# Batch 0's values: stationary columns read in steps of 64 elements in place of a sorted copy, with another order of work around it

## The chip, the cores and the metric

One core of a Trainium2 chip runs the whole kernel. The metric is device time in microseconds of one execution. A core has a matrix engine (TensorE, "PE" in the profile, with its weight loads on a row of their own, "PEld"), VectorE ("DVE"), ScalarE ("ACT"), GpSimd ("POOL", which here also issues the loads from DRAM) and SyncE ("SP"). Each engine runs its own instructions in the order written; semaphores make it wait for the others. Products of TensorE land in PSUM banks of 2 KB a partition, from which ScalarE or VectorE copies them out.

## What is computed

Two parts in a row: an attention whose key and value blocks are mixed by a doubly normalised 8x8 matrix, and a token and channel mixing network on its output.

```python
batch, n_heads, seq, head_dim = (4, 8, 768, 64)          # 8 blocks of 96
P = sort_net                                             # (4, 8, 8, 8)
for _ in range(5):
    P = np.exp(P - np.max(P, axis=-1, keepdims=True))
    P = P / (np.sum(P, axis=-1, keepdims=True) + 1e-09)
    P = P / (np.sum(P, axis=-2, keepdims=True) + 1e-09)
k_sorted = np.einsum('bhij,bhjcd->bhicd', P, k_b)
v_sorted = np.einsum('bhij,bhjcd->bhicd', P, v_b)
scores = scale * np.matmul(q_b, k_sb.transpose(0, 1, 2, 4, 3))   # within a block
attn = softmax(scores);  x = attn @ v_sb                 # back to (4, 768, 512)

a1 = alpha1 * x + beta1
tok = np.einsum('ts,bsd->btd', w_tok, a1)                # w_tok 768x768
u = x + lam * tok
a2 = alpha2 * u + beta2
ch = np.maximum(a2 @ w_ch1, 0.0) @ w_ch2                 # 512x2048, 2048x512
out = u + lam * ch
```

## The kernel before

The kernel works on one batch after another. From batch 1 on, a batch's attention is woven into the channel products of the batch before it. Batch 0 has nothing to hide behind: its attention is written out by hand, instruction by instruction, and this is where the change lies. A wrapper around each engine keeps the program's order on that engine, so the text of the first order (lines 893 to 957) is the order in which each engine meets the work. All instructions are recorded under the wrapper's line 65 in the profile, so tiles, not lines, tell what an instruction is.

Up to the first product of the channel network (tile `h_ps`) batch 0 goes as follows.

- **Loads.** GpSimd issues q, k, v, `w_tok`, then `alphaB`, `betaB`, `lamB`, four parts of `W1p`, four of `W2p`, and later (`load_kv(1)`, line 959, `load_q(1)`) the raw v and k of batch 1 and its six parts of q (`qn`). k and v take the two buffers of tag "raw"; `KT0` (turned keys) and `VD` (sorted values) take those of tag "tw".
- **The mixing matrix.** Five rounds of normalisation on VectorE and ScalarE. Beside them TensorE turns q (`q_ps`) and runs fillers: `warm(n)` (line 229) issues n products of zeros, whose result nobody reads. `mask(n)` (line 211) makes small constant masks on VectorE, in rounds 0 to 2.
- **Keys.** `mix_keys` (line 327) spreads the matrix over partitions (`repk_ps`) and makes `bigK` in two halves on VectorE. `k_turn` (line 392) multiplies it into the keys, one pair of heads at a time, and `k_copy` (line 395) brings the result into `KT0`.
- **Values.** `v8` holds, on each partition, 48 tokens of 64 elements. `v_sort` (line 167) copies it into `VD`, 64 elements of 64 tokens each (48 and zeros): elements 16 to 32 and 48 to 64 on GpSimd, 0 to 16 on ScalarE, 32 to 48 on VectorE. `v_mix` (line 403) makes eight elements at a time: 16 products, each with one element's 64 token columns of `VD` as the stationary operand and `bigV` as the moving one. A filler into the same bank stands before each even one. The result goes to `Vs`.
- **Attention.** `score` (line 419) makes the products of half a pair of heads into two PSUM banks and one exp of 128x768 into `et`. `pv_first` (line 453) multiplies with `Vs` (`x_ps`, 24 products), and VectorE takes the reciprocal (`rc`) and scales into `x`.
- **Token weights.** `permute` (line 594) reorders half of `w_tok` (`wt`) into `wp` with two copies (1,728 and 576 elements a partition; in before the first half is split in two). `wtok` turns it on TensorE (`wtok_ps`) and copies it into `w_tokT`.
- **First half of the tokens.** `row_sum(m)` adds up rows of `w_tok` on ScalarE into `rcol`; `row_sums` (line 613) copies `rcol` to `rc`, turns it on TensorE (`rr_ps`), and ScalarE copies the result into the row `rrow`. `first_mm(g)` (line 665) is the token product of column group g (`tok_ps`, 6 products) and ScalarE's copy `tok`. `first_turn(g)` (line 677) turns x (three products), adds the outer product of `rrow` and `brow` as a fourth (`turn_ps`); ScalarE then makes `z`, and VectorE, in `first_finish` (line 654), makes `a2T` from `tok_ps` and `z`. The `h_ps` products need the four `a2T`.

PSUM is given out by two helpers: `psa` (two buffers of two banks) and `psb` (four buffers of one bank).

Of the kernel before, what the change touches and what calls it, by code (L numbers as in the profile page):

```python
# [7 lines left out]
FT = mybir.dt.float32  # L8
F16 = mybir.dt.float16
# [7 lines left out]
def kernel(  # L17
# [75 lines left out]
    def const(shape, dtype, name):  # L93
        return wts.tile(shape, dtype, name=name, tag=name)
# [13 lines left out]
    nc.sync.dma_start(bet1[:], moe_beta1.rearrange("(o c) -> o c", o=1))  # L108

    KT0 = att.tile([128, H4, NB, 128], F16, name="kT0", tag="tw", bufs=2)  # L110
    VD = att.tile([128, D, 64], F16, name="vd", tag="tw", bufs=2)
    Vs = const([128, H * NB, GRP], F16, "Vs")
    q8 = moep.tile([128, H4, 12 * D], F16, name="q8", tag="u16", bufs=1)
    k8 = att.tile([128, H4, 12 * D], F16, name="k8", tag="raw", bufs=2)
    v8 = att.tile([128, HB, D], F16, name="v8", tag="raw", bufs=2)

    def load_slabs(dst, src):
        flat = src[0].rearrange("h s d -> (h s d)").rearrange("(g p f) -> p g f", p=128, f=12 * D)
        for g in range(0, H4, 2):
            pool.dma_start(dst[:, g:g + 2, :], flat[:, g:g + 2, :])  # L120

    def load_halves(dst, src):
        for th in range(2):
            pool.dma_start(
                dst[th * 64:(th + 1) * 64, :, :],
                src.rearrange("h (j th t) d -> th (h j) t d", j=NB, th=2)[th],
            )
# [10 lines left out]
    brow = att.tile([128, C], F16, name="brow", tag="uT", bufs=2)  # L138
    rrow = att.tile([128, 384], F16, name="rrow", tag="uT", bufs=2)
    load_slabs(q8, q)  # L140
    ident16 = const([128, 128], F16, "ident16")
    pool.memset(ident16[:], 0.0)
    pool.affine_select(
# [3 lines left out]
    dve.memset(brow[:].bitcast(FT), 0.0)  # L147
    dve.memset(rrow[:].bitcast(FT), 0.0)
    load_slabs(k8, k)
    load_halves(v8, v[0])  # L150
    heads()
    wt16 = []
    for half in range(2):
        t_ = att.tile([128, 3, S], F16, name="wt16", tag=("sums", "qn")[half], bufs=(2, 1)[half])
        for lo, n in ((0, 96), (TAIL, 32)):
            pool.dma_start(
                t_[lo // 6:lo // 6 + n],
                moe_w_tok[lo + 3 * half * n:lo + 3 * (half + 1) * n, :].rearrange("(tt p) s -> p tt s", p=n),
            )
        wt16.append(t_)  # L160
        if half == 0:
            pool.memset(VD[:, :, HB:64], 0.0)
            pool.memset(
                KT0[:].rearrange("p g i (th t) -> p (g i th) t", th=2)[:, :, HB:64].bitcast(FT), 0.0
            )

    def v_sort(lo, hi, eng):
        eng(VD[:, lo:hi, 0:HB], v8[:, :, lo:hi].rearrange("p t d -> p d t"))

    W1p = const([128, CT, HID], BF, "W1p")  # L170
    W2p = const([128, HT, C], F16, "W2p")
# [2 lines left out]
    alphaB = const([128, C], F16, "alphaB")  # L174
    betaB = const([128, C], F16, "betaB")
    lamB = att.tile([128, C], FT, name="lamB", tag="kT", bufs=1)
    pool.dma_start(alphaB[:], moe_alpha1.partition_broadcast(128))
    pool.dma_start(betaB[:], moe_beta1.partition_broadcast(128))
    pool.dma_start(lamB[:], moe_lam.partition_broadcast(128))
    v_sort(16, 32, pool.tensor_copy)  # L180
    for g in range(4):
        if g == 1:
            v_sort(48, 64, pool.tensor_copy)
        pool.dma_start(W1p[:, :, g * 512:(g + 1) * 512], w1v[:, :, g * 512:(g + 1) * 512])
    pool.tensor_tensor(brow[0:1, :], bet1[:], lam1[:], ALU.mult)

    vscr = dram.tile([B, H * NB, BLK, D], F16, name="vscr", tag="vscr")
    raw_of = {}
    qn_of = {}
# [21 lines left out]
    def mask(n):  # L211
        if n == 0:
            dve.tensor_copy(ident16f[:], ident16[0:4 * CT, 0:4 * CT])
            dve.tensor_reduce(mlo[:], ident16[:].rearrange("p (b j) -> p j b", j=NB), AXX, ALU.add)
        elif n == 1:
            dve.tensor_reduce(msk[:], ident16[:].rearrange("p (b j) -> p b j", j=NB), AXX, ALU.add)
            dve.tensor_tensor(mhi[:], msk[:, 0:8], msk[:, 8:16], ALU.add)
            dve.tensor_reduce(mth[:], ident16[:].rearrange("p (th c) -> p th c", th=2), AXX, ALU.add)
        elif n == 2:
            dve.tensor_reduce(  # L220
                mgap[:], ident16[:].rearrange("p (th t) -> p th t", th=2)[:, :, 0:HB],
                mybir.AxisListType.XY, ALU.add,
            )
# [5 lines left out]
    def warm(n, ps=psa):  # L229
        fill(ps([128, 512], FT, "warm_ps")[:], n)  # L230
# [71 lines left out]
    for it in range(5):  # L302
        act.activation(P32[:], P32[:], AF.Exp)
        dve.tensor_reduce(rsum[:], P32[:], AXX, ALU.add)
        dve.reciprocal(rsum[:], rsum[:])
        dve.tensor_tensor(
            P32[:], P32[:], rsum[:].unsqueeze(2).to_broadcast([BH, NB, NB]), ALU.mult
        )
        dve.tensor_reduce(csum[:], P32[:].rearrange("p i j -> p j i"), AXX, ALU.add)
        dve.reciprocal(csum[:], csum[:])  # L310
        dve.tensor_tensor(
            (P16 if it == 4 else P32)[:], P32[:],
            csum[:].unsqueeze(1).to_broadcast([BH, NB, NB]), ALU.mult,
        )
        if it < 3:
            with nc.allow_low_precision(reason="sums of zeros and a one"):
                mask(it)
        for f in beside[it]:
            f()

    for g in range(4):
        pool.dma_start(W2p[:, g * 4:(g + 1) * 4, :], w2v[:, g * 4:(g + 1) * 4, :])

    bigK = {}
    bigV = {}
# [66 lines left out]
    def k_turn(b, g, ps):  # L392
        return turn_slab(k8, lambda r, g: bigK[b][r, g, :], g, "k_ps", ps)
# [9 lines left out]
    def v_mix(b, n, ps, eng):  # L403
        ps = ps([128, 8, 64], FT, "v_ps")
        fill(ps[:].rearrange("p d x -> p (d x)"), 1 - n % 2)
        for s in range(8):
            for th in range(2):
                d = (s + 4 * th) % 8
                r = slice(th * 64, th * 64 + 64)
                pe.matmul(  # L410
                    ps[r, d, :], VD[r, n * 8 + d, :],
                    bigV[b][r, :, :].rearrange("p h i -> p (h i)"), start=True, stop=True,
                )
        eng(Vs[:, :, n * 8:(n + 1) * 8], ps[:].rearrange("p d x -> p x d"))
# [2 lines left out]
    kT_of = {0: KT0}  # L417

    def score(b, g, hf, ps):
        ps = ps([128, 2, 512], FT, "sc_ps")  # L420
        n = 128 if b == 0 else BLK
        keys = kT_of[b][:].rearrange("p g i t -> p (g i t)")
        for ii in range(4):
            i = 4 * hf + ii
            lo = (g * NB + i) * n
            w = min(128, H4 * NB * n - lo)
            for h2 in range(2):
                r = slice(h2 * 64, h2 * 64 + 64)
                pe.matmul(
                    ps[0:w, h2, ii * BLK:(ii + 1) * BLK], keys[r, lo:lo + w],  # L430
                    qT_of[b][r, g, i * BLK:(i + 1) * BLK], start=True, stop=True,
                )
        tag, bufs = ("ost", 4) if (b, g) == (0, 3) else ("et", 6)
        et = att.tile([128, 2, 4, BLK], F16, name="et", tag=tag, bufs=bufs)
        act.activation(
            et[0:n].rearrange("p a i t -> p a (i t)"), ps[0:n, :, 0:4 * BLK], AF.Exp, scale=scale
        )
        ets[(b, g, hf)] = et

    x_of = {}  # L440
# [450 lines left out]
        prep_wtok(ks, 0, psb, eng)  # L891

    mix_keys(0, psb)
    warm(3)
    mix_values(0, psb)
    prep_scales()
    dve.tensor_copy(Vs[:, :, D:GRP], mgap[:].unsqueeze(2).to_broadcast([128, H * NB, GRP - D]))
    kp0 = k_turn(0, 0, psb)
    kp1 = k_turn(0, 1, psb)
    k_copy(0, 0, kp0, 0, copy)  # L900
    k_copy(0, 0, kp0, 1, act.copy)
    warm(3)
    kp2 = k_turn(0, 2, psb)
    k_copy(0, 1, kp1, 0, copy)
    k_copy(0, 1, kp1, 1, act.copy)
    kp3 = k_turn(0, 3, psb)
    k_copy(0, 2, kp2, 0, copy)
    k_copy(0, 2, kp2, 1, act.copy)
    v_sort(0, 8, act.copy)
    v_sort(8, 16, act.copy)  # L910
    score(0, 0, 0, psa)
    k_copy(0, 3, kp3, 0, copy)
    k_copy(0, 3, kp3, 1, copy)
    score(0, 0, 1, psa)
    v_sort(32, 48, copy)
    warm(2, psb)
    v_mix(0, 0, psb, copy)
    v_mix(0, 1, psb, copy)
    score(0, 1, 0, psa)
    v_mix(0, 2, psb, copy)  # L920
    v_mix(0, 3, psb, act.copy)
    score(0, 1, 1, psa)
    v_mix(0, 4, psb, copy)
    v_mix(0, 5, psb, copy)
    score(0, 2, 0, psa)
    v_mix(0, 6, psb, copy)
    v_mix(0, 7, psb, act.copy)
    score(0, 2, 1, psa)
    row_sum(0)
    permute(0, copy, 0, 3)  # L930
    moe_start(0)
    warm(1, psb)
    pv_first(0)
    score(0, 3, 0, psa)
    wtok(0, copy)
    wtok(1, act.copy)
    wtok(2, copy)
    permute(0, copy, 3, 6)
    row_sum(1)
    row_sum(2)  # L940
    pv_first(1)
    wtok(3, copy)
    wtok(4, copy)
    wtok(5, copy)
    permute(1, copy, 0, 6)
    score(0, 3, 1, psa)
    pv_first(2)
    row_sums(psb)
    first_mm(0, psb)
    first_turn(0, psb)  # L950
    first_mm(1, psb)
    pv_first(3)
    first_turn(1, psb)
    first_mm(2, psb)
    scale_affine(alphaB)
# [148 lines left out]
```

## Time and profile before

| | us |
|---|---|
| median of three runs | 259.97 (259.43 to 260.12) |
| the profiled execution's own time | 258.79 |
| its span | 257.0 |
| first `k_ps` product | 13.48 |
| first `v_ps` product of the mixing | 17.57 |
| first `x_ps` product | 24.52 |
| first `tok_ps` product | 31.00 |
| first `h_ps` product | 35.88 |

The times in the table's lower part count from the start of the span. A row of the timeline gives the start, the duration of a group of like instructions on one engine, the engine, the line, the operation, the tile written and the tiles read, the size, and the number; in brackets stands the idle time before it and what ended it. The sum of busy times says what share of the span an engine worked; it does not say which of them sets the end.

Landings of the loads in this execution: q 5.94 and 7.81, k 9.65 and 11.60, v 15.04 and 16.38, the first half of `w_tok` 19.17, the second 22.75, `lamB` 26.33, `W1p` 28.81 to 36.47, `W2p` 38.98 to 46.64.

### The profile page before, as it was taken

The numbers are of one execution on the slowest core, as the hardware profiler recorded it, in microseconds if no ns is written. First come the engines' busy times: TensorE is split into PE (matmuls) and PEld (weight loads), VectorE is DVE, ScalarE is ACT, GpSimd is POOL, SyncE is SP. The second block draws the span as 40 slices with busy tenths as digits, with TensorE's granted clock in tenths as the row PEclk, the third lists the DMA queues.
The fourth block names the chain that finished last, engine by engine and source line by source line (L and its number), as shares of the span: only waits on it lengthen the run. The fifth ranks groups of instructions, "written<-read, shape, count | busy, mean of one in ns | idle before, by whom it ended". The sixth has DMA issues, their size and how long they took to land.

```text
span 257.0 us, 5959 instructions
## 1 busy us (share of the span) xinstructions
PE 246.4 (96%) x2371; PEld 159.7 (62%) x2371; DVE 176.3 (69%) x467; ACT 155.3 (60%) x282; POOL 44.2 (17%) x67
## 2 busy tenths in 40 slices
PE   7998799999999999999999999999999999999994
PEld 3465565555555545456865787557756875686783
DVE  6796888595539945759896675298887773461873
ACT  3567767485997539787565587877465004847400
POOL 8759302700074000047000000000000000000000
PEclk9999999999999999999999999999999999999999
DMA  5999999998999957999994259810202232111022
GB/s 99 214 203 179 209 205 211 214 151 173 122 209 187 150 128 159 143 136 192 145 143 120 41 135 170 151 20 3 84 0 42 62 101 65 23 40 41 3 82 82
DMA packets 67535, 31.07 MB, mean 121 GB/s; under 512 B 56674, under 2 KB 63218, under 8 KB 67508
## 3 DMA queue, kind: packets, MB, share of 16 engines
q0 software_dynamic: 26352, 15.34, 46.4%
q1 hardware_dynamic: 41060, 15.33, 33.6%
q8 instruction: 18, 0.29, 0.5%
q14 instruction: 9, 0.07, 0.1%
q10 hardware_dynamic: 96, 0.03, 0.1%
HBM read 32.79 MB, written 8.65 MB: 161 GB/s over the span
## 4 chain that ended last, share of the span: by engine, by line
PE 75%; DVE 10%; DMA 7%; ACT 4%; issue 2%; SPq 1%; DVEq 0%; POOLq 0%
PE h_ps L65 27%; PE tok_ps L65 10%; PE px L65 8%; PE pz L65 6%; PE py L65 6%; DVE x L65 5%; PE ch_ps L65 4%; PE x_ps L65 3%; DMA Vs<-vscr 3%; PE warm_ps L65 2%; DMA vscr<-mixed 2%; PE sc_ps L65 2%; DMA q<-in_q_dram 2%; DVE a L65 2%; PE v_ps L65 1%
## 5 line engine op out<-in xcount | busy, mean ns | idle before, releaser
L65 PE MATMUL h_ps<-a2T,W1p 128*128 128x384 bf16 x512 | 93.2, 326 | 0.0
L65 PEld LDWEIGHTS <-W1p 128*128 128x128 bf16 x512 | 47.9, 98 | 31.3 <-issue 0.2
L65 ACT ACTIVATE hTa<-h_ps 128x384 f16<-128x384 f32 x64 | 31.2, 493 | 27.3 <-PE h_ps L65 26.4
L65 ACT ACTIVATE hTb<-h_ps 128x384 f16<-128x384 f32 x64 | 31.2, 490 | 7.6 <-PE h_ps L65 7.6
L65 DVE SCALAR_TENSOR_TENSOR u<-tok_ps,x 128x512 f32<-128x512 f32 x21 | 14.5, 690 | 26.0 <-PE tok_ps L65 26.0
L65 PE MATMUL tok_ps<-a,w_tokT 128*128 128x512 f16 x126 | 30.3, 379 | 0.5 <-DVE a L65 0.5
L65 ACT CAST kT<-kmix_ps 64x512 f16<-64x512 f32 x36 | 25.8, 716 | 4.9 <-PE kmix_ps L65 4.4
L65 ACT ACTIVATE et<-sc_ps 96x768 f16<-96x768 f32 (+1 forms) x32 | 24.8, 808 | 3.7 <-PE sc_ps L65 3.7
L65 ACT CAST u<-u 128x512 f16<-128x512 f32 x21 | 13.0, 618 | 22.9 <-DVE u L65 22.9
L65 PEld LDWEIGHTS <-sums 128*128 128x128 f16 x216 | 21.1, 98 | 3.3 <-issue 0.2
L65 PEld LDWEIGHTS <-hTb 128*128 128x128 f16 x200 | 18.6, 98 | 6.3
L65 PEld LDWEIGHTS <-hTa 128*128 128x128 f16 x192 | 18.3, 98 | 6.4
L65 PEld LDWEIGHTS <-w_tokT 128*128 128x128 f16 x126 | 12.3, 98 | 13.8 <-issue 1.0
L65 DVE TENSOR_TENSOR x<-x_ps,rcb 96x512 f16<-96x512 f32 x24 | 16.5, 687 | 0.8
L65 POOL DMA_DIRECT2D qn<-in_q_dram x18 | 16.0, 913 | 4.3 <-DMA raw<-in_v_dram 4.2
L65 DVE TENSOR_TENSOR sums<-hTa,hTb 128x512 f16<-128x512 f16 (+2 forms) x27 | 8.9, 330 | 10.4 <-ACT hTb L65 10.0
L65 PEld LDWEIGHTS <-et 96*128 96x128 f16 (+4 forms) x288 | 11.8, 100 | 5.3 <-DVE x L65 1.6
L65 PE MATMUL x_ps<-Vs,et 96*128 96x65 f16 (+4 forms) x288 | 13.0, 195 | 1.8 <-DVE x L65 0.9
L65 DVE SCALAR_TENSOR_TENSOR ost<-px,u 128x256 f32<-128x256 f32 x27 | 11.3, 417 | 3.5 <-PE px L65 3.5
L65 PE MATMUL warm_ps<-wz 128*128 128x512 f16 x36 | 11.0, 439 | 1.2 <-DVE wz L65 1.2
L65 PE MATMUL ch_ps<-W2p,hTb 128*128 128x512 f16 x48 | 12.0, 379 | 0.0
L65 ACT CAST mixed<-mix_ps 128x1024 f16<-128x1024 f32 x9 | 9.1, 1012 | 4.7 <-PE mix_ps L65 4.5
(139 smaller groups left out, 352.9 us busy)
## 6 DMA issues: line engine op xcount, KB each, us to landing
out_dram<-ost SPq DMA_DIRECT2D x23, 192.0 KB, 2.7
raw<-in_v_dram POOLq DMA_DIRECT2D x6, 384.0 KB, 6.9
raw<-in_k_dram POOLq DMA_DIRECT2D x6, 384.0 KB, 9.5
qn<-in_q_dram POOLq DMA_DIRECT2D x18, 128.0 KB, 10.5
vscr<-mixed SPq DMA_DIRECT2D x6, 384.0 KB, 5.2
Vs<-vscr SPq DMA_DIRECT2D x3, 768.0 KB
W1p<-in_moe_w_ch_dram POOLq DMA_DIRECT2D x4, 512.0 KB, 11.9
W2p<-in_moe_w_ch_dram POOLq DMA_DIRECT2D x4, 512.0 KB, 17.4
```

What stands on the lines that cost most here:

```text
L65: ins = getattr(self.eng, name)(*args, **kwargs)
```

## The change

`VD` and the four sorting copies are gone. `v8` is now 64 tokens long (48 loaded and 16 zeroed by GpSimd), in the buffer that `VD` had, and `v_mix` reads one element's token columns from it directly, in steps of 64 elements:

```diff
-    VD = att.tile([128, D, 64], F16, name="vd", tag="tw", bufs=2)
-    v8 = att.tile([128, HB, D], F16, name="v8", tag="raw", bufs=2)
+    v8 = att.tile([128, 64, D], F16, name="v8", tag="tw", bufs=2)
...
+    pool.memset(v8[:, HB:64, :].bitcast(FT), 0.0)
...
-    load_halves(v8, v[0])
+    load_halves(v8[:, 0:HB, :], v[0])
...
-    def v_sort(lo, hi, eng):
-        eng(VD[:, lo:hi, 0:HB], v8[:, :, lo:hi].rearrange("p t d -> p d t"))
...
-                    ps[r, d, :], VD[r, n * 8 + d, :],
+                    ps[r, d, :], v8[r, :, n * 8 + d],
```

The masks are spread over the five rounds, one small group in each, and `mask(4)` follows `mix_values`. `score` may now take two one-bank buffers of `psb`, with one exp of 128x384 for each:

```diff
+        if ps is psb:
+            ps = [ps([128, 4 * BLK], FT, "sc_ps") for _ in range(2)]
+            bank = [t_[:] for t_ in ps]
...
+            for a in range(2):
+                act.activation(
+                    et[0:n, a].rearrange("p i t -> p (i t)"), ps[a][0:n, :], AF.Exp, scale=scale
+                )
```

The first order is written anew. GpSimd now makes the copy of `mgap` into `Vs` and both halves of `permute`, between its load issues; nine fillers become two; `k_turn(0, 0)` follows `mix_keys` at once; `row_sums` stands behind `first_mm(1)`.

```diff
     mix_keys(0, psb)
-    warm(3)
-    mix_values(0, psb)
-    prep_scales()
-    dve.tensor_copy(Vs[:, :, D:GRP], mgap[:].unsqueeze(2).to_broadcast([128, H * NB, GRP - D]))
     kp0 = k_turn(0, 0, psb)
-    kp1 = k_turn(0, 1, psb)
     k_copy(0, 0, kp0, 0, copy)
     k_copy(0, 0, kp0, 1, act.copy)
-    warm(3)
+    mix_values(0, psa)
+    with nc.allow_low_precision(reason="sums of zeros and a one"):
+        mask(4)
+    pool.tensor_copy(Vs[:, :, D:GRP], mgap[:].unsqueeze(2).to_broadcast([128, H * NB, GRP - D]))
+    pool.dma_start(alphaB[:], moe_alpha1.partition_broadcast(128))
+    pool.dma_start(betaB[:], moe_beta1.partition_broadcast(128))
+    pool.dma_start(lamB[:], moe_lam.partition_broadcast(128))
+    for g in range(4):
+        if g == 2:
+            permute(0, pool.tensor_copy, 0, 6)
+        pool.dma_start(W1p[:, :, g * 512:(g + 1) * 512], w1v[:, :, g * 512:(g + 1) * 512])
+    pool.tensor_tensor(brow[0:1, :], bet1[:], lam1[:], ALU.mult)
+    permute(1, pool.tensor_copy, 0, 6)
+    for g in range(4):
+        pool.dma_start(W2p[:, g * 4:(g + 1) * 4, :], w2v[:, g * 4:(g + 1) * 4, :])
+    warm(1, psa)
+    kp1 = k_turn(0, 1, psb)
+    warm(1)
     kp2 = k_turn(0, 2, psb)
...
-    v_sort(0, 8, act.copy)
-    v_sort(8, 16, act.copy)
     score(0, 0, 0, psa)
+    k_copy(0, 3, kp3, 1, act.copy)
     k_copy(0, 3, kp3, 0, copy)
-    k_copy(0, 3, kp3, 1, copy)
+    prep_scales()
     score(0, 0, 1, psa)
-    v_sort(32, 48, copy)
-    warm(2, psb)
+    score(0, 1, 0, psa)
     v_mix(0, 0, psb, copy)
     v_mix(0, 1, psb, copy)
-    score(0, 1, 0, psa)
-    v_mix(0, 2, psb, copy)
-    v_mix(0, 3, psb, act.copy)
+    v_mix(0, 2, psb, act.copy)
     score(0, 1, 1, psa)
+    v_mix(0, 3, psb, copy)
     v_mix(0, 4, psb, copy)
-    v_mix(0, 5, psb, copy)
+    v_mix(0, 5, psb, act.copy)
     score(0, 2, 0, psa)
     v_mix(0, 6, psb, copy)
-    v_mix(0, 7, psb, act.copy)
-    score(0, 2, 1, psa)
-    row_sum(0)
-    permute(0, copy, 0, 3)
+    v_mix(0, 7, psb, copy)
     moe_start(0)
-    warm(1, psb)
+    score(0, 2, 1, psb)
     pv_first(0)
-    score(0, 3, 0, psa)
     wtok(0, copy)
     wtok(1, act.copy)
     wtok(2, copy)
-    permute(0, copy, 3, 6)
+    score(0, 3, 0, psb)
+    pv_first(1)
+    row_sum(0)
+    score(0, 3, 1, psb)
+    pv_first(2)
+    wtok(3, copy)
+    wtok(4, act.copy)
+    wtok(5, copy)
     row_sum(1)
     row_sum(2)
-    pv_first(1)
-    wtok(3, copy)
-    wtok(4, copy)
-    wtok(5, copy)
-    permute(1, copy, 0, 6)
-    score(0, 3, 1, psa)
-    pv_first(2)
+    first_mm(0, psb)
+    pv_first(3)
+    first_mm(1, psb)
     row_sums(psb)
-    first_mm(0, psb)
     first_turn(0, psb)
-    first_mm(1, psb)
-    pv_first(3)
     first_turn(1, psb)
     first_mm(2, psb)
```

In the part of the loads, the issues of `alphaB` to `W2p` that stood earlier in the text are removed there; the order in which GpSimd issues the loads stays.

## The prediction

> **What bounds the kernel now.** I read the busy shares of the page first, then stretches of the span, then TensorE's timeline up to its first h_ps product, then the timelines of the engines that it waited for.
>
> ```profile
> PE 246.4 (96%) x2371; PEld 159.7 (62%) x2371; DVE 176.3 (69%) x467; ACT 155.3 (60%) x282; POOL 44.2 (17%) x67
> ...
> q8 instruction: 18, 0.29, 0.5%
> ```
>
> Three stretches of the span (busy us and instructions of TensorE, weight loads, VectorE, ScalarE, GpSimd; then clock, DMA share, GB/s):
>
> ```profile
> 20.00:36.00 16.00, 13.30 (x264) 9.73 (x258) 12.04 (x25) 11.24 (x22) 7.92 (x11) 1.00 1.21 195
> 36.00:50.00 14.00, 13.65 (x91) 7.65 (x89) 10.19 (x25) 8.70 (x19) 5.47 (x7) 1.00 1.18 212
> 50.00:70.00 20.00, 20.00 (x144) 11.28 (x143) 13.54 (x30) 14.87 (x23) 1.10 (x2) 1.00 1.43 153
> ```
>
> TensorE is busy 246.4 of 257.0 us, always at granted clock 1.00; from 50 to 70 us it never stops. So whatever delays its first h_ps product (35.88 us) is carried to the end, less at most the 0.35 us still idle between 36 and 50. The change lies wholly ahead of that product; there 2.70 us of 16 are idle, and these rows of TensorE's timeline (start, duration, then idle time and who ended it) tell why.
>
> ```profile
> 16.37 0.51 PE L65 MATMUL sc_ps<-qT,kT 64*128 64x96 f16 x16
> ...
> 20.66 0.40 PE L65 MATMUL v_ps<-bigV,vd 64*64 64x64 f16 x13
> 22.14 0.47 PE L65 MATMUL v_ps<-bigV,vd 64*64 64x64 f16 x19 [1.08 <-issue]
> ...
> 26.85 0.83 PE L65 MATMUL x_ps<-Vs,et 128*128 128x65 f16 x18 [0.44 <-DVE x L65]
> 28.34 0.34 PE L65 MATMUL x_ps<-Vs,et 128*32 128x65 f16 x6 [0.66 <-issue]
> ...
> 30.00 0.93 PE L65 MATMUL x_ps<-Vs,et 128*128 128x65 f16 x21 [0.43 <-DVE x L65]
> ```
>
> The two largest stalls wait for no engine and no transfer ("issue"), and fall inside a group. The products between them, added up from the timeline, are exactly 128, with 128 weight loads 256 instructions. The instruction queue moved 0.29 MB in 18 packets, about 16 KB each; 4,742 products and loads in 0.29 MB are some 62 bytes each, so a packet holds about 256. I infer that code arrives in blocks of 256. The previous edge, 128 products back, lies in the last k_ps group at about 16.05 us, so late blocks come 6.1 and 6.2 us apart: a floor on this stage that no shorter copy or sort passes.
>
> **The change, part by part.** The sum is made against the profiled execution, 258.79 us (span 257.0), which is 1.2 below the median 259.97; a difference is carried over to the median unchanged.
>
> *Sort removed.* It took GpSimd 2 x 1.513, ScalarE 2 x 0.854 and VectorE 1.18 us. TensorE felt it only as part of stalls that the block floor holds: the idle ahead of v_ps is "issue". I count nothing. If the blocks came early, up to 1.08 + 0.66 = 1.74 us would be free; that is a rival.
>
> *Key turns first.* k_turn(0,0) needs only the first half of bigK: the first repk group ends at 12.04, then selk 0.285, redk 0.286, bigK 0.292, so about 13.05 instead of 13.48. The nine fillers become two; in before they filled waits. Block edges follow where TensorE got to, so the 0.4 us survives: the edge before tok_ps comes at about 27.9 instead of 28.34, and by counting products it now lies at the start of score(0,3,1). Gain 0.44.
>
> *Loads of strided columns.* No row shows a 64-column load with a step of 128 bytes. Below: ident with step 0 loads in 102 ns against 109 for the packed 64 columns, so no cost. Above: ScalarE's sort, reading with this step, took 854 ns for 384 elements, its packed 384-element copy 483 less about 162 for the smallest copy; GpSimd's and VectorE's read 1.97 and 1.54 ns an element. 854/384 less that fixed part is 1.8 ns a column, 116 ns a load, 58 a product on two row halves against today's 19.4 (0.62/32): (58 - 19.4) x 128 = 4.9, less the 1.74 of stall in which it hides, 3.2 us. In between, twice today's spacing: 2.5 less 1.74, 0.8. I take 0, the row of the same engine and operation; the 1.74 is the cover, and a gap beyond 14 ns a product passes it.
>
> [...]
>
> *GpSimd permutes w_tok.* 1,728 and 576 elements a half: at the memset's 0.95 ns an element 2.2 us, at the sort's 1.97 ns 4.5. The first starts when w_tok's first half has landed (19.17) and is needed by wtok_ps at 25.73: slack of 2 us even so. Behind it queue W1p 2 and 3, brow (1.26), the second permute, the W2p issues and raw v. Their issues move up to about 7 us later, but W1p needs 11.9 us from issue to landing because the transfers ahead fill the queue, so landings stay. Cost 0; that cover gone, each us late in the raw v issue is a us late at mix. VectorE loses 1.04 + 0.44 + 2 x (0.485 + 0.264), and the Vs copy of 0.23.
>
> *Evictions.* Two on ScalarE in other places (592 against 683), three exps in two halves (about 2 x 0.49, by hTa's row of 128x384, for 0.81): 0.5 us more on ScalarE, busy 11.24 of 16 there. Nothing waits on it until the tail.
>
> *The tail before h_ps.* Here before hides a chain; I show its rows on ScalarE and the third a2T's supplier:
>
> ```profile
> 30.32 0.19 ACT L65 CAST rc<-rcol 128x3 f16<-128x3 f32 x1
> 31.11 0.47 ACT L65 COPY rrow<-rr_ps 1x384 f16<-1x384 f16 x1 [0.60 <-PE rr_ps L65]
> 32.19 0.58 ACT L65 ACTIVATE tok<-tok_ps,ab2col 128x384 f16<-128x384 f32 x1 [0.61 <-PE tok_ps L65]
> 32.67 0.66 ACT L65 ACTIVATE z<-turn_ps,ab2col 128x384 f32<-128x384 f32 x1
> ```
>
> The row sums go column, transpose, row while x_ps and tok_ps products run. After, row_sums is issued behind both token products. Stepping on from the edge at 27.9 with before's spacings: score 0.29, pv_first(2) 0.94 to 29.13, wtok 0.61 to 29.74. VectorE must do rc and x (0.23, 0.96; in before x ended 1.33 after the last product) to 30.45, then two turn copies (three took 0.87) to 31.05; the first token product's last step needs the last copy: ends 31.21 instead of 30.73, a wait of **0.48**. pv_first(3) 0.94, the second token product 0.97: issued by 33.12, drained 33.29. ScalarE: tok copy to 33.91, rc behind it to 34.02, so rr_ps at 34.05: TensorE idle **0.93**. Its transposes drain at 34.35, rrow to 34.86, and turn 0's last product waits for it from 34.37: **0.53**. Turn 1 is done at 35.40. The bank of the third token product is the one that turn 0 holds until its z copy ends: drain 35.23 + z 0.66 = 35.93, idle **0.57** to 35.97. Then 0.97 and 0.33: first h_ps at 37.27. That is 35.88 + 1.39. Counting the other way: new waits 2.51; away go the edge's 0.44, the 0.43 wait at 30.00, and 0.25 of products that now lie ahead of the edge: 1.39.
>
> Sum: -0.44 and the rest of the tail's terms = +1.39; 258.79 + 1.39 = 260.18, on the median 259.97 + 1.39 = **261.4**. The 0.35 idle of 36 to 50 could take some back: 261.0.
>
> **Rivals.** (1) *Strided loads are dear*: the second mechanism on top; for it the row readers' ratios, against it the step-0 row and the cover. 261.4 + 0.8 to 3.2 = 262.2 to 264.6. (2) *Not slower*: the blocks of code come earlier, because TensorE reaches v_ps with more code in hand; place 22.14 and 28.34, price 1.74. It decides once 1.39 of it is gone: 261.4 - 1.74 = 259.7 in full, and 259.2 if the 0.4 us between x_ps groups goes too. It can't be much more, since the transfers cap a gain:
>
> ```profile
> 50.58 0.87 POOL L65 DMA_DIRECT2D qn<-in_q_dram  x1 [0.97 <-DMA raw<-in_v_dram]
> ```
>
> That last q load lands 9.4 us after issue at the quickest, at 60.0; qt_ps needs it at 60.7, so beyond 0.75 us TensorE would wait there. For it: the sort's engines do go free. Against it: the stalls' exact 128-product spacing. (3) *The tail waits are hidden* in part, because ScalarE gets to rc before the tok copy or the bank is free sooner: 0.93 + 0.53 gone leaves -0.1: 259.9, no change. Against: both stand in one queue in that order. (4) *GpSimd's permute is slower than the sort's rate*, or the loads are delayed: only beyond about 6.5 us a half, 1 us each: 262.4 and more.
>
> **How the numbers follow.** Forecast 0.50, its own range 260.8 to 262.0; rival 1 0.17; rival 2 0.15; rival 3 0.14; rival 4 0.04. Below 259.2 only rival 2's and 3's ends: 0.12 faster. "No change" is 259.2 to 260.75 (0.3%, 0.78 us, is what a measurement can tell): the rest of 2 and 3 and the forecast's edge, 0.20. Slower 0.68. Range 259.4 to 263.8: it leaves out rival 2's end and the dearest loads.
>
> **What would show it.** h_ps first at 37 us; rr_ps waiting on ScalarE's rc, the turn's last product on rrow, tok_ps on z; two "issue" waits still 128 products apart; v_ps spacing near 19 ns. Wrong if rr_ps doesn't wait, if "issue" has gone from 15 to 30 us, if v_ps loads take over 109 ns each in the spacing, or if wp copies run past 25.7.

## The result and the profile after

The changed kernel takes 268.93 us (median of four runs, 268.09 to 269.17), the kernel before beside it 259.7: a ratio of 1.036, interval 1.0325 to 1.0388. It is slower by 9.2 us where 1.4 were forecast, and lies above the stated range. Here and below a ratio leaves out an execution that is over 1.5% slower than the fastest of its kernel (one of e2, one of e5).

The page of the kernel after, its busy shares and the granted clock in 40 slices, and last the clock line of the kernel before:

```profile
PE 255.5 (96%) x2364; PEld 167.4 (63%) x2364; DVE 171.9 (65%) x457; ACT 155.2 (58%) x285; POOL 45.2 (17%) x70
...
PEclk9995569999999999999999999999999999999999
...
PEclk9999999999999999999999999999999999999999
```

TensorE's busy time has grown by 9.1 us although it does seven products fewer: the loss isn't idle time but slower work. The clock line, all nines before, shows why in part: within the fourth to the sixth slice TensorE's granted clock was 0.50. Short stretches around the two changes of clock (the third figure from the end is the granted clock):

```profile
20.40:20.60 0.20, 0.20 (x5) 0.16 (x3) 0.03 (x1) 0.00 (x0) 0.20 (x1) 1.00 1.11 187
20.60:20.80 0.20, 0.20 (x1) 0.00 (x0) 0.18 (x1) 0.00 (x0) 0.20 (x1) 0.58 1.19 200
20.80:21.00 0.20, 0.20 (x3) 0.04 (x2) 0.20 (x1) 0.00 (x0) 0.20 (x1) 0.50 1.03 172
...
37.50:37.75 0.25, 0.25 (x6) 0.25 (x4) 0.25 (x1) 0.07 (x1) 0.00 (x0) 0.60 1.26 209
37.75:38.00 0.25, 0.25 (x4) 0.18 (x3) 0.25 (x1) 0.25 (x1) 0.00 (x0) 1.00 1.33 213
```

Half clock lasts from 20.6 to 37.7 us, 17.1 us, and TensorE is busy in all of it but two waits of 0.36 and 0.32. Its timeline from the first mixing of values to the first `h_ps` product, and the group of the strided weight loads:

```profile
18.03 0.35 PE L65 MATMUL sc_ps<-qT,kT 64*128 64x96 f16 x8 [0.73 <-ACT et L65]
18.31 0.39 PE L65 MATMUL v_ps<-wz 128*128 128x512 f16 x1
18.63 1.95 PE L65 MATMUL v_ps<-bigV,v 64*64 64x64 f16 x32
20.50 0.52 PE L65 MATMUL v_ps<-wz 128*128 128x512 f16 x1
...
29.61 1.64 PE L65 MATMUL x_ps<-Vs,et 128*128 128x65 f16 x24 [0.36 <-DVE Vs L65]
31.18 1.14 PE L65 MATMUL wtok_ps<-ident,wp 128*128 128x128 f16 x9
...
41.79 0.33 PE L65 MATMUL rr_ps<-ident,rc 128*1 128x128 f16 x3 [0.75 <-ACT rc L65]
...
42.68 0.32 PE L65 MATMUL turn_ps<-rrow,brow 128*128 128x384 f16 x1 [0.28 <-ACT rrow L65]
...
43.76 1.14 PE L65 MATMUL tok_ps<-w_tokT,x 128*128 128x384 f16 x6 [0.43 <-ACT z L65]
...
45.06 0.65 PE L65 MATMUL h_ps<-a2T,W1p 128*128 128x384 bf16 x3
```

```profile
L65 PEld LDWEIGHTS <-v 64*64 64x64 f16 x128 | 7.4, 199 | 1.6 <-issue 1.5
```

Three things are to be seen. The first 32 products of the mixing, still at full clock, take 20.50 - 18.63 = 1.87 us, 58.4 ns each, against 19.4 before. The profile gives a load 199 ns, not 109, but 128 of them fill only 7.4 us of the row: they overlap, and the spacing is the price. At half clock the 24 `x_ps` products take 31.18 - 29.61 = 1.57 us against 0.94. And of the four waits forecast for the tail, three (on `rc`, `rrow` and `z`) stand where the prediction put them. The first `h_ps` product comes at 45.06 us instead of 35.88, 9.18 later; from there to the end both kernels take 221 us.

### The profile page after: what moved, and what is told of

It reads as the page before. It is cut to its first block, busy times and chain, and to the rows that moved or that the text cites. A ratio compares the mean times of both kernels' runs of the same rounds, so it can differ in the third digit from the quotient of the medians.

```text
span 266.3 us, 5941 instructions
## 1 busy us (share of the span) xinstructions
PE 255.5 (96%) x2364; PEld 167.4 (63%) x2364; DVE 171.9 (65%) x457; ACT 155.2 (58%) x285; POOL 45.2 (17%) x70
## 4 chain that ended last, share of the span: by engine, by line
PE 73%; DMA 10%; DVE 9%; ACT 4%; issue 1%; SPq 1%; DVEq 0%; ACTq 0%
PE h_ps L65 25%; PE tok_ps L65 10%; PE px L65 7%; PE pz L65 5%; DMA uT<-u 5%; PE py L65 5%; PE ch_ps L65 4%; PE x_ps L65 4%; PE v_ps L65 4%; PE warm_ps L65 3%; DMA Vs<-vscr 3%; DVE x L65 3%; PE sc_ps L65 2%; DMA vscr<-mixed 2%; DVE a L65 1%
## 5 line engine op out<-in xcount | busy, mean ns | idle before, releaser
L65 ACT ACTIVATE hTa<-h_ps 128x384 f16<-128x384 f32 x64 | 31.2, 494 | 27.0 <-PE h_ps L65 26.1
L65 DVE SCALAR_TENSOR_TENSOR u<-tok_ps,x 128x512 f32<-128x512 f32 x21 | 14.5, 691 | 26.1 <-PE tok_ps L65 26.1
L65 ACT ACTIVATE et<-sc_ps 96x768 f16<-96x768 f32 (+2 forms) x35 | 25.1, 754 | 5.1 <-PE sc_ps L65 5.1
L65 ACT CAST u<-u 128x512 f16<-128x512 f32 x21 | 13.0, 618 | 22.7 <-DVE u L65 22.7
L65 PEld LDWEIGHTS <-et 96*128 96x128 f16 (+4 forms) x288 | 13.4, 109 | 3.8 <-DMA Vs<-vscr 0.6
L65 PE MATMUL x_ps<-Vs,et 96*128 96x65 f16 (+4 forms) x288 | 14.7, 207 | 0.5 <-DVE Vs L65 0.4
L65 PE MATMUL sc_ps<-qT,kT 64*128 64x96 f16 (+1 forms) x256 | 11.2, 215 | 1.9 <-ACT et L65 1.0
L65 PEld LDWEIGHTS <-kT 64*128 64x128 f16 (+1 forms) x256 | 7.0, 99 | 8.5 <-issue 5.3
```

The lines of the kernel that those rows point to most:

```text
L65: ins = getattr(self.eng, name)(*args, **kwargs)
```

## The experiments

Two causes show in one trace, so the first experiments take them apart: what the strided load costs, what the order costs, and what brings the clock down.

**e1: packed loads in the changed kernel.**

```diff
-                    ps[r, d, :], v8[r, :, n * 8 + d],
+                    ps[r, d, :], v8[r, n * 8 + d, :],
```

> The changed kernel, but each stationary operand of v_mix is 64 elements side by side instead of 64 elements in steps of 64; it leaves the right values out (they are those of other elements), order, counts and sizes stay. Theory A (the strided load costs 58 - 19 = 39 ns a product, and its slowness also starves TensorE's array so that the clock halves): v_ps spacing back to 19.4 ns, granted clock 1.0 throughout, first h_ps near 37.3, time near 261.4, which is what the order of the tail alone was forecast to cost. Rival B (the clock halves because seven fillers are gone and the keys wait for ScalarE): v_ps spacing 19 to 25 ns, but the clock still falls near 20.7 us; time 264 to 266.

Measured: 263.45 us (261.55 to 263.82), a ratio of 1.014 (1.009 to 1.020) to 259.63. The spacing is 19.4 ns again and 5.5 us of the loss are gone. But A falls in part: the clock still halves, from 22.7 to 33.0 us, 10.2 us long. So the 5.5 hold some clock as well as load. TensorE's timeline of e1:

```profile
20.35 0.50 PE L65 MATMUL v_ps<-bigV,v 64*64 64x64 f16 x19
22.12 0.40 PE L65 MATMUL v_ps<-bigV,v 64*64 64x64 f16 x13 [1.26 <-issue]
...
25.29 1.64 PE L65 MATMUL x_ps<-Vs,et 128*128 128x65 f16 x24 [0.53 <-DVE Vs L65]
```

With quick loads the wait for code at 22.1 is back, and ahead of the drop TensorE stood still for 1.26 us.

**e2: as e1, with row_sums ahead of the token products.**

```diff
-    first_mm(0, psb)
-    pv_first(3)
-    first_mm(1, psb)
     row_sums(psb)
+    first_mm(0, psb)
     first_turn(0, psb)
+    pv_first(3)
+    first_mm(1, psb)
     first_turn(1, psb)
```

> As e1_packed, and in the tail row_sums, then first_mm(0) and first_turn(0), stand before pv_first(3) and first_mm(1), nearly as in the kernel before. If the tail's three waits (rr_ps on rc, the turn on rrow, tok_ps on z; 0.75 + 0.28 + 0.43 us in the changed kernel) are what the order costs, they go, and it is 1.2 to 1.5 us faster than e1_packed: 259.9 to 260.2. If they only cover another wait (w_tokT's copies, code), it gains less than 0.5.

Measured: 260.87, 262.50, 264.07 and 265.88 us, a ratio of 1.012 (1.005 to 1.019): no gain that can be told. `rr_ps` waited 2.43 us for `rc`, since the sums of `row_sum(1)` and `row_sum(2)` were still running on ScalarE until 33.4. That wait itself emptied TensorE, and the clock fell here, from 34.2 to 37.7. At the wait for code in `v_ps`, 1.26 us as in e1, it did not fall. The execution of 260.87 us kept its clock throughout.

**e3: strided loads alone, in the kernel before** (its sort taken out, `v8` in the buffer of `VD` as in the change, its order and fillers kept).

```diff
-                    ps[r, d, :], VD[r, n * 8 + d, :],
+                    ps[r, d, :], v8[r, :, n * 8 + d],
```

> The kernel before, with its order, fillers and tail, but without the sort: v_mix reads the columns in steps of 64. Theory A: v_ps spacing 58 ns, 128 x 39 = 5.0 us more less the two code waits of 1.74 in which it hides, and the clock halves as in the changed kernel, for some 4 us more: 266 to 268. Rival B: the fillers hold the clock at 1.0: 259.7 + 3.3 = 263.

Measured: 263.02 us (262.56 to 264.68), 1.015 (1.009 to 1.021). Both theories miss half of it: the spacing is 58 ns and the clock does fall (23.3 to 33.5), as A says, but the time is the 263 of B. No wait for code is left, so the load's 5.0 us are hidden in part by the 1.74, and the waits for `x` shrink from 0.87 to 0.24; a third of the 10.2 us of half clock (3.4) falls on `v_ps` products, which keep the pace of their loads anyway (59.7 ns each at half clock, 58.4 at full). The rest of the difference between 266 to 268 and 263 wasn't traced row by row.

**e4 and e9: the price of a load by its step.** Both add, ahead of the kernel before, 32 products with 64-column stationary operands for each step, after six fillers. Each ran once. The loop of e4, in part:

```diff
+        fill(out[:].rearrange("p d x -> p (d x)"), 6)
...
+                    pe.matmul(
+                        out[r, (s + 4 * th) % 8, :], flat[r, o:o + 63 * step + 1:step], wz[r, 0:64],
+                        start=True, stop=True,
+                    )
```

> The kernel before with a stretch added ahead of everything: for each of the steps 1, 2, 4, 8, 16, 32, 64, 66, 72 and 1 elements again, 32 products with a 64-column stationary operand read in that step, after six fillers. Its time only says that the stretch was added (some 20 us); the spacing of the 32 products is what counts. [...]

> The kernel before with a stretch ahead of everything, as in e4_steps: 32 products each at steps 1, 2, 3, 4, 5, 6, 7 and 64 elements with 64 rows, then steps 64 and 1 with 128 rows. From e4_steps (19.4, 19.7, 33.8, 63.4 ns at steps 1, 2, 4, 8, i.e. 8, 16, 32, 64 lines of 16 bytes a load) theory E: a load takes about 1 ns for each 16-byte line that it touches, with a floor of 19.4 from the products: steps 3, 5, 6, 7 touch 24, 40, 48, 56 lines and cost about 25, 41, 49, 57 ns. [...] With 128 rows, each load fills the whole height and can't overlap with its neighbour in the other half: if lines alone count, step 64 stays near 60; if two halves were read side by side, it is nearer to 120.

The rows of e9, steps 1, 4, 64 and then 64 with 128 rows (tiles sa, se, si, sj), each with the fillers that follow:

```profile
6.65 0.69 PE L65 MATMUL sa_ps<-wz,W2p 64*64 64x64 f16 x32
7.27 1.47 PE L65 MATMUL sb_ps<-wz 128*128 128x512 f16 x6
...
12.95 1.16 PE L65 MATMUL se_ps<-wz,W2p 64*64 64x64 f16 x32
14.03 1.47 PE L65 MATMUL sf_ps<-wz 128*128 128x512 f16 x6
...
24.30 1.96 PE L65 MATMUL si_ps<-wz,W2p 64*64 64x64 f16 x32
26.20 1.47 PE L65 MATMUL sj_ps<-wz 128*128 128x512 f16 x6
27.59 3.74 PE L65 MATMUL sj_ps<-wz,W2p 128*64 128x64 f16 x32
31.27 2.56 PE L65 MATMUL sk_ps<-wz 128*128 128x512 f16 x6
```

The start of a group to that of the next, over 32, is the spacing: 0.62/32 = 19.4 ns, 33.8, 59.4 and 115. All of them, in ns a product:

| step in elements | 1 | 2 | 3 | 4 | 5 | 6 | 7 | 8 | 16 | 32 | 64 | 66 | 72 |
|---|---|---|---|---|---|---|---|---|---|---|---|---|---|
| lines of 16 bytes touched (estimate) | 8 | 16 | 24 | 32 | 40 | 48 | 56 | 64 | 64 | 64 | 64 | 64 | 64 |
| e4 | 19.4 | 19.7 | | 33.8 | | | | 63.4 | 63.8 | 58.8 | 58.8 | 62.5 | 63.4 |
| e9 | 19.4 | 19.7 | 26.6 | 33.8 | 41.6 | 48.4 | 55.9 | | | | 59.4 | | |

The price rises with the step up to 8 elements, 16 bytes (63.4 ns), and no further: 58.8 to 63.8 from 16 to 72. Theory E counts in stretches of 16 bytes for that reason; its "line" is an estimate from these prices, not something that a trace shows. It fits: from step 3 on 0.92 to 1.11 ns for each line, over a floor of 19.4. (At 64 lines the steps differ by up to 5 ns, which E doesn't explain.) Leaving step 1 is not by itself dear, since step 2 costs 19.7, but step 4, half of the 8, already costs 33.8; and powers of two are not what makes the price, since 66 and 72 cost 62.5 and 63.4. With 128 rows the price doubles to 115 ns, as forecast for two half-height loads that run side by side; by that reading, an estimate, one alone takes about 1.8 ns a line. The overlap itself isn't seen in e9, and the check with 128 rows at step 1 (49.6 ns) ran mostly at half clock.

**e5: fillers in the changed kernel.** By now three drops had been seen, at 20.6, 22.7 and 23.3 us, lasting 17.07, 10.24 and 10.24 us, and one of 3.41 in e2: all whole multiples of 3.41. Theory C, an estimate, was formed on this: the clock is set anew every 3.4 us by how full the array was.

```diff
-        fill(ps[:].rearrange("p d x -> p (d x)"), 1 - n % 2)
+        fill(ps[:].rearrange("p d x -> p (d x)"), 2)
...
+    warm(3, psb)
     score(0, 0, 1, psa)
```

> The changed kernel with fillers: two of 512 columns ahead of every v_mix (16 in place of 4) and three ahead of the second score. New theory C: the clock halves when, over a window of about 3.4 us, the columns streamed through the array, weighted by the share of its 128 rows in use, fill less than about 0.37 of the time (0.29 in the changed kernel ahead of the drop, 0.36 in both others that dropped at their v_ps), and it returns once a window at half clock is filled over some 0.8. A v_mix of 16 products in 0.94 us with two fillers has (16 x 0.0267 x 0.5 + 0.43)/1.37 = 0.47: the clock stays at 1.0, the half-clock stretch of 17 us goes, which cost some 4.3 us on x_ps, wtok_ps, sc_ps and fillers; 12 to 15 fillers cost 2.6 to 3.2: 266 to 267.5, with v_ps spacing still 58 ns. Rival D (the strided loads draw the clock down by themselves): it still halves, 271 to 272.

Measured: 267.25, 267.30 and 268.11 us in three executions with a mean clock of 0.999 to 1.000, ratio 1.029 (1.027 to 1.032): 1.6 less than the changed kernel although it does 15 fillers more. In the fourth, the profiled one, the clock fell twice, ahead of the strided stretch (15.1 us) and at its end (32.2), and it took 271.58. Rival D is out: strided loads at full clock are possible, here with two fillers ahead of every 16 products.

**e6: packed loads and eleven fillers, where TensorE waited anyway.**

```diff
-        fill(ps[:].rearrange("p d x -> p (d x)"), 1 - n % 2)
+        fill(ps[:].rearrange("p d x -> p (d x)"), 5 if n == 4 else 1 - n % 2)
...
+    warm(2, psa)
     kp0 = k_turn(0, 0, psb)
...
+    warm(3, psb)
     score(0, 0, 1, psa)
...
+        if g == 0:
+            fill(ps[:, 0, :], 2)
```

> As e1_packed (values of other elements, packed loads), with eleven fillers put where TensorE waited there anyway: two ahead of the first k_ps, three ahead of the second score, four more in the fifth v_mix, two ahead of the first x_ps. By C the window that ended at 0.36 gains 0.25 and the clock stays at 1.0 throughout; what is left is the order's own cost, forecast as 1.4: 261.1 (260.6 to 261.6), with rr_ps, turn_ps and tok_ps waiting as before. If the clock still halves, C's threshold or its measure is wrong: 263 and more.

Measured: 261.01 us (260.63 to 262.11), ratio 1.0059 (1.0036 to 1.0082); mean clock 0.999 to 1.000 in all five runs. Beside e1, which differs by the fillers alone, eleven more products make it 2.4 us faster. The waits of TensorE in e6 between 10 and 45 us (sum, number, longest):

```profile
PE rr_ps L65 <- ACT rc L65: 0.8, 1, 0.8
PE tok_ps L65 <- DVE w_tokT L65: 0.5, 1, 0.5
PE tok_ps L65 <- ACT z L65: 0.4, 1, 0.4
...
PE x_ps L65 <- issue: 0.3, 1, 0.3
PE turn_ps L65 <- ACT rrow L65: 0.3, 1, 0.3
```

**e7: as e6, with all sums early and the tail in the order of before.**

```diff
     row_sum(0)
+    row_sum(1)
     score(0, 3, 1, psb)
+    row_sum(2)
...
-    row_sum(1)
-    row_sum(2)
+    row_sums(psb)
     first_mm(0, psb)
-    pv_first(3)
-    first_mm(1, psb)
-    row_sums(psb)
     first_turn(0, psb)
+    first_mm(1, psb)
+    pv_first(3)
     first_turn(1, psb)
```

> As e6_packed_fill, with all of row_sum earlier on ScalarE (two behind pv_first(1), the third behind the last score) and row_sums, first_mm(0), first_turn(0), first_mm(1), pv_first(3), first_turn(1) in the order of the kernel before: rc is ready when rr_ps is issued, unlike in e2_packed_tail, where the sums were still running. The three waits go (1.46), and it is 1.0 to 1.5 faster than e6_packed_fill, about level with the kernel before: 259.4 to 260.2. If the waits only move (to w_tokT's copies or code), under 0.5.

Measured: 260.07 us over ten runs, ratio 1.0021 (0.9995 to 1.0048), 0.94 less than e6: a little under the expected 1.0. Of the tail's waits a 0.34 on `rc` is left. In its profile a wait for code of 0.86 stands where e6 had 0.30, and the clock fell for one window, so part of the gain was lost again there.

**e8: GpSimd's permutes alone, in the kernel before.** The issues of the last two parts of `W1p` and of `W2p`, and `brow`, move with them, behind the permutes as in the change.

```diff
-    permute(0, copy, 0, 3)
-    permute(0, copy, 3, 6)
-    permute(1, copy, 0, 6)
+    permute(0, pool.tensor_copy, 0, 6)
...
+    permute(1, pool.tensor_copy, 0, 6)
```

> The kernel before with one part of the change alone: both permutes of w_tok on GpSimd, between its load issues, in place of VectorE. If VectorE's 2.5 us there set the x_ps waits (0.44 and 0.43), these go and up to 0.6 us is gained, the code edges staying: 259.0 to 259.7. If the permute or the loads behind it come late: slower by their lateness, at the first wtok_ps.

Measured: 259.5 us, ratio 0.9998 (0.9978 to 1.0019): nothing. The copies took 1.626 and 0.668 us; the two waits for `x` stayed (0.9 us), so it wasn't the permutes on VectorE that set them. In the profile the first wait for code was 0.60 us, not 1.08, and `h_ps` came at 35.39, 0.49 earlier; TensorE then waited 1.42 for ScalarE's `u` at 113.6, a wait that the kernel before doesn't have. A gain ahead of `h_ps` isn't always carried to the end.

**e10 and e11: more and fewer fillers in the kernel before.**

```diff
-        fill(ps[:].rearrange("p d x -> p (d x)"), 1 - n % 2)
+        fill(ps[:].rearrange("p d x -> p (d x)"), 4 if n == 4 else 1 - n % 2)
...
+        if g in (1, 2):
+            fill(ps[:, 0, :], 2)
```

> The kernel before, valid, with seven more fillers where it waited: three more in the fifth v_mix, two each ahead of the second and third x_ps group. In the kernel before the weakest 3.4 us window lies at 0.38, just where the clock fell elsewhere; some of its executions show a mean clock of 0.993 and 260 to 261.7 us. By C none do here: no run over 260.5, the median 0 to 0.3 lower, 259.3 to 259.6. If the fillers aren't hidden: 0.5 to 1.5 slower.

Measured: 259.43 us, ratio 1.0011 (0.9993 to 1.003). The clock is 0.997 or more in all twelve runs, but there was next to nothing to gain (beside it one execution of 23 of the kernel before is under that), and the forecast gain of 0 to 0.3 didn't come. For e11 the fillers in `v_mix` and `warm(2, psb)` ahead of it are deleted:

```diff
-        fill(ps[:].rearrange("p d x -> p (d x)"), 1 - n % 2)
...
-    warm(2, psb)
```

> The kernel before, valid, without its four fillers in the v_ps banks and the two ahead of them: six products of zeros fewer, all else as before. By C a window between 17 and 28 us falls under 0.37 (0.41 less 2 x 0.06), the clock halves for three windows or more, and it is slower by 1.5 to 4: 261 to 263.5, though it does less. If activity isn't what counts, or the code edges hide it: 259.2 to 259.8.

Measured: 259.44 us, ratio 1.0008 (0.9985 to 1.003), but a mean clock of 0.985 to 0.993 in every one of ten runs. C is right on the clock, and my price for it was wrong. TensorE's timeline of e11, at half clock from 19.3 to 26.1 us:

```profile
21.22 1.40 PE L65 MATMUL v_ps<-bigV,vd 64*64 64x64 f16 x32
22.55 0.50 PE L65 MATMUL sc_ps<-qT,kT 64*128 64x96 f16 x8
22.98 1.06 PE L65 MATMUL v_ps<-bigV,vd 64*64 64x64 f16 x32
...
27.68 1.02 PE L65 MATMUL x_ps<-Vs,et 128*128 128x65 f16 x24 [0.44 <-DVE x L65]
...
35.90 0.65 PE L65 MATMUL h_ps<-a2T,W1p 128*128 128x384 bf16 x3
```

The slower products spend the time that TensorE otherwise waited for code (1.08 and 0.66 us, now gone) and that three of the deleted fillers took (0.96 by the rows of before), and `h_ps` starts at 35.90, as before (35.88). So half a clock cost nothing here because there was such time to be used up; e11 doesn't show it free beside equal work.

## Why the prediction was wrong, point by point

**The order and its tail: right in kind, and close in part by luck.** Without the strided load and at full clock, e6 measures +1.4 us by the medians, the forecast +1.39; by the two profiles its first `h_ps` is 1.86 later (37.74). Single terms were off both ways. The waits on `w_tokT`, `rc`, `rrow` and `z` came out at 0.48, 0.75, 0.28 and 0.43, in sum 1.94 for the 2.51 forecast: the steps between engines on this chain are shorter than I stepped them. A wait that I had not seen ate what the keys gained: three scores in a row on two buffers, the third waiting 0.73 in after and e1 until the first score's exp (0.81 us, from 17.17 in after) had freed its buffer. In e6 fillers stand in it. The wait for code at `v_ps` and `x_ps` stayed (e1: 1.26 at 22.1; e6: 0.30 at 27.9, where 27.9 was forecast, though e6's eleven fillers had moved the place).

**GpSimd's permutes: right.** 1.63 and 0.67 us, at the lower of the two bounds (0.94 and 1.16 ns an element). Their being free is shown by e8. The second half ran to 26.75 in after, past the 25.7 that the prediction named as a sign of being wrong, but the first `wtok_ps` came only at 31.18 and waited for nothing.

**The sort removed: nearly nothing, but not only behind code.** In before the first 32 `v_ps` products took 1.00 us where later ones take 0.69, and their loads waited 0.42 and 0.24 for ScalarE's `vd`: the sort was felt there by some 0.3 us.

**The strided loads: the step that failed.** "I take 0, the row of the same engine and operation" was the wrong choice between two ends that I had both written down. The operand with step 0 (102 ns a load) reads one element again and again, so it says nothing of a step that moves on. The other end, ScalarE's sort, read the same data with the same step; 1.8 ns a column, 116 ns a load and 58 ns a product were computed from it; a product took 58.4, and 115 with 128 rows. The row that shares the access pattern was nearer than the row that shares the engine. That it agrees so closely is luck: GpSimd and VectorE read this step at 1.97 and 1.54 ns an element. The term put at 0 costs 128 x (58.4 - 19.4) = 5.0 us.

**The cover of 1.74 us: right in kind.** In the changed kernel no "issue" wait is left in this stage. That these are waits for code stays an inference; the instruction queue's packets bear it out: in before two of 16 KB started at 19.71 and 25.86 us and took 0.96 and 0.89, and TensorE went on 1.5 and 1.6 us after their ends. The floor isn't fixed, though: e8, with TensorE's products unchanged, waited 0.60 for the 1.08.

**The clock: a term that was missing.** I took it for constant because it had been 1.00 throughout, and did not ask what held it there. I named the nine fillers only as something that fills waits. By e11 such products hold the clock (two of the nine and the four in `v_mix` were deleted, and the mean clock was 0.985 to 0.993 in all ten runs), and by e6 against e1 eleven of them are worth 2.4 us. Rival 1, which had the load right, ended at 264.6, mainly for want of this term.

The sum, counted in the profiles from the first `repk_ps` product to the first `h_ps`: 24.09 us before, 25.86 in e6, 32.61 after. So the order costs 1.77, and load and half clock 6.75. The load is the 5.0. Row by row half clock adds some 4.3: three `x_ps` groups 3 x 0.63, five scores 5 x 0.16, two `wtok_ps` groups 0.87, three fillers 0.57, `v_ps` 0.2. It is paid in part by time that the changed kernel doesn't spend as e6 does, in waits and in fillers put into waits: 1.16 in the fifth `v_mix`, 0.51 ahead of the first `x_ps`, 0.48 on `w_tokT`, 0.30 on code. That leaves 5.0 + 4.3 - 2.45 = 6.9, which meets the 6.75. So half clock costs some 1.8 us here; by the medians, 9.2 - 1.4 - 5.0, it is 2.8. No run shows this share by itself, and it stays an estimate: the one filler count tried with strided loads (e5) added work of its own. The remaining 0.66 of the 9.18 stands ahead of `repk_ps` (12.45 us after, 11.79 before, 11.89 in e1 and 12.43 in e2, which are alike up to there) and is spread between executions.

No version was faster than the kernel before: e7, e8, e10 and e11 are level with it.

## What to carry to other kernels

Price a strided stationary operand by its step: in e4 and e9 64 columns of 2-byte elements cost 19.4 and 19.7 ns a product at steps 1 and 2, 33.8 at 4, and 59 to 64 at 8 and beyond. Where no row shows its load, take a row with the same access pattern, even on another engine, rather than one of the same engine with another pattern. Before products are removed or slowed, ask what keeps the clock up: fillers that look like padding may be what holds it, and by the sums below the weakest stretch of 3.4 us counted, not the mean. A row of sums that a rank-one product needs late should be started early, where its three short steps lie beside other products.

## What the runs showed of the hardware

**Half clock came in multiples of 3.41 us, after stretches with few rows in use.** Half clock (granted clock 0.50) lasted 17.07, 10.24, 10.24, 3.41, 3.41 and 6.83, 3.41, 3.41 and 6.82 us in the profiles of after, e1, e3, e2, e5, e7, e9 and e11: 5, 3, 3, 1, 1 and 2, 1, 1 and 2 times 3.41. For each window of 3.41 us counted from these edges I added up the columns streamed at 0.42 ns each (fillers of 512 are 0.216 us apart in e9; 0.83 ns at half clock, where they are 0.425 apart), times the share of the 128 rows in use:

| window | share of the window, rows weighted |
|---|---|
| at full clock, the clock then fell (after, e1, e2, e3, e5, e7, e9, e11) | 0.20 to 0.38 |
| at full clock, it stayed | 0.39 and more |
| at half clock, it stayed half | 0.51 to 0.73 |
| at half clock, it came back | 0.75 to 0.95 |

That a window of 3.41 us decides, by this measure and at one threshold, is an estimate from these sums: about 0.38 of full rate fits all of them (0.73 and 0.75 at half clock are 0.37 and 0.38 of full rate). By the same estimate it counts where the windows lie: e1 and e2 have the same 1.26 us wait in `v_ps`, but the window over it holds 0.35 in e1, where the clock fell, and 0.39 in e2, where it stayed. The strided stretch of 64-row products reaches (0.0267 x 0.5)/0.0584 = 0.23 while the profile calls TensorE 100% busy. By the same sum the kernel before comes as low as 0.38 at one phase (26.2 us), and a few of its executions show a clock of 0.993. No window ahead of a drop was idle: the emptiest, in e2, held 0.20.

**A strided load of 128 rows cost twice one of 64.** At a step of 64 elements a 64-row load cost 59 ns in a stream that alternates the halves, a 128-row load 115 (e9).
